# A planner that gives out all eight PSUM banks piece by piece, in a kernel of an FFT convolution and a gated MLP

## The chip, the cores and the metric

The kernel runs on one core of one Trainium2 chip. The core has five engines: TensorE (PE, with its weight loads shown apart as PEld), VectorE (DVE), ScalarE (ACT), GpSimd (POOL) and SyncE (SP, which here only issues DMAs). The metric is the device time of one execution in microseconds (us).

## The reference

Two blocks follow one another on an input u of 2048 positions and 512 channels. All is float32.

```
x   = layernorm(u)
dt  = exp(log_dt);  A = -exp(log_A_real) + 1j*A_imag
K   = 2 * real(sum_n  C[d,n]*dt[d] * exp(A[d,n]*dt[d] * l))     # a filter of 2048 taps for each of 512 channels, 128 modes n
y   = irfft(rfft(x, 4096) * rfft(K, 4096))[:2048]
h   = u + y + x * D_skip
z   = gelu(layernorm(h) @ w_in);  z1, z2 = halves of z
out = h + (z1 * (w_sp @ layernorm(z2) + b_sp)) @ w_out
```

## The kernel before, in words

The first block is `phase_a`, the second the phases `b1`, `b2` and `b3`. The change lies in `phase_a` alone.

**The work of phase a.** The 512 channels are handled in four chunks of 128. For each chunk, eight *units* (`unit`, line 619) make the filter: two matmuls give phases in PSUM (`ph`), ScalarE and VectorE reduce them to a fraction of a turn, ScalarE takes sines and cosines, GpSimd makes three products of amplitudes (`m`, in the tile `wa`), VectorE multiplies amplitudes with sines and cosines, TensorE sums over the modes, and ScalarE copies the result into `ks`. A unit's tiles appear in the profile as `f`, `ph`, `ce`, `wb` (the buffers `cs`) and `wa` (the buffers `m`).

The convolution is cut in *pieces*, eight of each kind for a chunk: `piece_a` (line 707) is the first step of the transform of the input and `piece_b` the second, whose result is `ka`; `kb` is a copy of `ka` with its halves exchanged, made by DMA. `piece_c` (line 719) is the first step of the transform of the filter, into a quarter of `big` called `x1k`. `piece_d` is the second step and multiplies it into `ka` and `kb`. It goes by groups of frequencies, so it needs all eight pieces c of its chunk. `piece_e` (line 727) is the inverse, by groups of four channels. Each piece is some matmuls into one PSUM bank and an evacuation by ScalarE (a, b, c, e) or two multiplications by VectorE (d).

Before this come `norm_x` (the layer norm: 64 normalizing operations, given out to ScalarE, VectorE and GpSimd by the string `NORM`, lines 503 to 522) and `params` (line 539: some 40 small operations on 128 x 128 elements, for chunks 0 and 1 alone and for 2 and 3 together). `table` and `stack` load what the units of the next chunk need.

**The order of the work.** `phase_a` does not issue instructions; it hands them to `Plan` (line 178) with a due time for each (`nc.at`). `Plan` has a cost for every operation, builds a list schedule, improves it by going forwards and backwards, shakes the due times at random 60 times (`TRIES`), keeps the best, and issues the instructions in that fixed order, engine by engine. A cost model of the engines stands in `_add`; it knows that VectorE and GpSimd exclude each other in some operations (`port`). All these instructions bear line 424 in the profile.

**PSUM.** It has eight banks of 512 float32 per partition. `phase_a` fixes four for `ph` (two units of two banks), one for the second cosine `ce`, and leaves three (`FFT_BUFS`) for the planner to give to pieces. The filter sums of a unit go into the first half of its `ph`.

**The hand-over.** What stands after the last use of the units' tiles is not issued in `phase_a` but by `rest`, from `phase_b1` (line 818), behind the loads of that phase. After the first inverse piece of the last chunk the weights of the next phase are split (lines 808 and 809, tiles `w1h` and `w1l`).

Of the kernel before, what the change touches and what calls it, by code (L numbers as in the profile page):

```python
# [26 lines left out]
NORM = "aavaapav"  # L27
# [4 lines left out]
TRIES = 60  # L32
# [145 lines left out]
class Plan:  # L178
# [4 lines left out]
    HOP = 0.2  # L183

    def __init__(self, nc, banks):
        self.nc, self.banks, self.ops, self.live, self.t, self.step = nc, banks, [], {}, 0.0, 0.0
        self.nbank, self.open = 0, None
        for e in self.ENGINES:
            setattr(self, e, _Engine(self, e))
# [4 lines left out]
    def bank(self, shape):  # L194

        self.nbank += 1
        n = math.prod(shape[1:])
        names = "abc"[:len(shape) - 1]
# [5 lines left out]
    def group(self, dur):  # L204

        self.open = dict(calls=[], aps=[], eng=None, dur=dur)
        yield
        g, self.open = self.open, None
        self._add(**g)

    def _resolve(self, x, bank=None):
        return x.view(self.banks[0] if bank is None else bank) if isinstance(x, Late) else x

    def call(self, e, method, args, kw, dur=None):
# [10 lines left out]
        return self._add(calls, aps, e, dur)  # L225

    def _add(self, calls, aps, eng, dur):
        e, method, args, kw = calls[0]
        o = dict(id=len(self.ops), eng=self.ENGINES[eng], calls=calls, t=self.t, deps={}, banks=set(), func=None, lat=0.0)
        self.t += self.step  # L230
        o["port"] = False
        views = [(self._resolve(x), w) for x, w in aps]
        spaces = [str(v.space) for v, _ in views]
        out, ins = views[0][0], [v for v, w in views[1:] if math.prod(v.shape[1:]) > 1]
        n = math.prod(out.shape[1:])
        isps = ["PSUM" in str(v.space) for v in ins]
        if o["eng"] == "DVE":
            ins = ins or [out]
            two = method not in ("tensor_scalar", "tensor_scalar_add", "tensor_scalar_mul", "tensor_copy", "memset", "bn_stats",
                                 "reciprocal")  # L240
            c = math.prod(ins[0].shape[1:]) if method == "bn_stats" else n
            ps = any(isps) or "PSUM" in str(out.space)
            if two or ps or method == "bn_stats":
                d = 0.15 + c / 960
            elif method == "reciprocal":
                d = 0.15 + c / 160
            else:
                d = 0.15 + c / 1920
            o["port"] = not ps and method not in ("bn_stats", "reciprocal", "memset")
        elif o["eng"] == "ACT":  # L250
            d = 0.18 + n * 0.00083
            f = str(args[2]).split(".")[-1] if method == "activation" else "Copy"
            o["func"] = {"Exp": "exp", "Sin": "sin", "Arctan": "sin"}.get(f)
        elif o["eng"] == "POOL":
            d, o["port"] = 0.3 + n * 0.0022, True
        elif o["eng"] == "PE":
            d = 0.4
        else:
            d = 0.06
        if method == "dma_start":  # L260
            nb = 4 * out.shape[0] * n if out.shape else 0
            o["lat"] = 2.0
            o["dma"] = nb / 250e3
            o["port"] = False
            if o["eng"] == "POOL":
                d = 0.7
        o["dur"] = dur if dur is not None else d
        for (x, w), (v, _) in zip(aps, views):
            key = x.key if isinstance(x, Late) else v.tensor.name
            if isinstance(x, Late):  # L270
                o["banks"].add(x.key)
            if isinstance(key, str) and key.startswith("in_"):
                continue
            self._touch(o, key, v, w)
        o["names"] = {v.tensor.name for v, _ in views}
        self.ops.append(o)
        return o
# [27 lines left out]
    def prepare(self):  # L305
# [8 lines left out]
        for ids in holders.values():  # L314
            for i in ids[1:]:
# [9 lines left out]
    def list_schedule(self, want, back=False):  # L325
# [9 lines left out]
        ready, free = {e: [] for e in engines}, {e: 0.0 for e in engines}  # L335
        est, start, end = [0.0] * n, [0.0] * n, [0.0] * n
        banks, held, until, uses = [(0.0, i) for i in range(len(self.banks))], {}, {}, dict(self.uses)
        port = dma = last = 0.0
        table = None
        for i in range(n):  # L340
            if not left[i]:
                ready[ops[i]["eng"]].append(i)
        for _ in range(n):
            best = None
            for e in engines:
                cand = []
                for i in ready[e]:
                    t = max(est[i], free[e])
                    if i in self.bank_of and self.bank_of[i] not in held:
                        if not banks:  # L350
                            continue
                        t = max(t, min(banks)[0])
                    if ops[i]["port"]:
                        t = max(t, port)
                    cand.append((t, i))
                if cand:
                    soon = min(cand)[0] + 0.25
                    w, i, t = min((want[i], i, t) for t, i in cand if t <= soon)
                    if best is None or (t, w, i) < best:
                        best = (t, w, i)  # L360
            t, _, i = best
            o = ops[i]
            e = o["eng"]
            ready[e].remove(i)
            b = self.bank_of.get(i)
            if b is not None and b not in held:
                x = min(banks)
                banks.remove(x)
                held[b] = x[1]
            d = o["dur"]  # L370
            if o["func"] and o["func"] != table:
                d, table = d + 1.28, o["func"]
            start[i], end[i] = t, t + d
            free[e] = end[i]
            if o["port"]:
                port = end[i]
            done = end[i]
            if "dma" in o:
                dma = max(dma, end[i]) + o["dma"]
                done = dma + o["lat"]  # L380
            last = max(last, done)
            if b is not None:
                uses[b] -= 1
                until[b] = max(until.get(b, 0.0), end[i])
                if not uses[b]:
                    banks.append((until[b] + self.HOP, held[b]))
            for x in after[i]:
                left[x] -= 1
                est[x] = max(est[x], done + (0.0 if ops[x]["eng"] == e and "dma" not in o else self.HOP))
                if not left[x]:  # L390
                    ready[ops[x]["eng"]].append(x)
        return last, start, end, held

    def improve(self, want, rounds):

        best = None
        for _ in range(rounds):
            last, start, end, held = self.list_schedule(want)
            if best is None or last < best[0]:
                best = (last, want, start, held)  # L400
            _, _, back, _ = self.list_schedule([-x for x in end], True)
# [3 lines left out]
    def schedule(self, tries):  # L405
        self.prepare()
        rnd = random.Random(1)
        best = self.improve([o["t"] for o in self.ops], 8)
        for _ in range(tries):
            s = rnd.choice([0.5, 1.0, 2.0])  # L410
            new = self.improve([x + rnd.gauss(0.0, s) for x in best[1]], 4)
            best = min(best, new, key=lambda b: b[0])
        last, _, start, held = best
        for o in self.ops:
            o["bank"] = held.get(self.bank_of.get(o["id"]))
        return sorted(self.ops, key=lambda o: (start[o["id"]], o["id"])), last, start

    def issue(self, o):
        def real(x):
            return x.view(self.banks[o["bank"]]) if isinstance(x, Late) else x  # L420
# [17 lines left out]
def phase_a(ctx, gen, tc, ins, cst, ident, c_mean, c_inv, Q, wp, scr):  # L438
# [12 lines left out]
    x1, kab = one(w1, "x1", [SLOT]), [one(w1, t, [SLOT]) for t in ("ka", "kb")]  # L451
# [41 lines left out]
    pm1 = Carve(kab[1])  # L493
# [8 lines left out]

    def norm_x(half, al, t0, t1):
# [5 lines left out]
        mean, rstd, nmr = group_norm(nc, al, bank, st, 32, c_mean, f"lnx{half}")  # L509
        nc.at(t1, 0.3)  # L510
        xo = big[:, 0::3, :].rearrange("p h (x l) -> p h x l", x=64)
        for j in range(32):
# [3 lines left out]
            e = NORM[j % len(NORM)]  # L516
            if e == "a":
                nc.scalar.activation(o, i, AF.Identity, bias=nmr[:, j:j + 1], scale=rstd[:, j:j + 1], dur=0.58)
            else:
                eng = nc.gpsimd if e == "p" else nc.vector  # L520
                eng.tensor_scalar(o, i, mean[:, j:j + 1], rstd[:, j:j + 1], op0=ALU.subtract, op1=ALU.mult,
                                  dur=1.05 if e == "p" else 0.47)
# [16 lines left out]
    def params(al, c0, n, rt):  # L539

        N = n * NS
# [5 lines left out]
        ai, cr, ci = (rt[:, i].rearrange("p c s -> p (c s)") for i in range(3))  # L547
        a, b, mx, mn, ph, c_, t, th = (al(N) for _ in range(8))
# [3 lines left out]
        for c in range(n):  # L552
            s_ = slice(NS * c, NS * c + NS)
            nc.scalar.activation(th[:, s_], ai[:, s_], AF.Identity, scale=ndt[:, c0 + c:c0 + c + 1])
# [7 lines left out]
        nc.scalar.activation(dummy, half_pi, AF.Sin)  # L562
# [16 lines left out]
        nc.vector.scalar_tensor_tensor(ph, pr[:, 2], -31.5, ph, op0=ALU.mult, op1=ALU.add)  # L579
        rounded(ph)  # L580
        nc.vector.scalar_tensor_tensor(pr[:, 0], t, MAGIC, ph, op0=ALU.subtract, op1=ALU.subtract)
# [587 lines left out]
```

## Time and profile before

| | us |
|---|---|
| three executions, median | 989.69 |
| lowest and highest | 985.25, 992.40 |
| the profiled execution, its own time | 990.94 |
| its span, first to last instruction | 989.2 |
| TensorE busy, of the span | 866.9 |
| VectorE | 546.4 |
| ScalarE | 397.2 |
| GpSimd | 230.1 |
| granted TensorE clock, mean | 0.974 |

Busy time is the time in which an engine has an instruction in it, and an instruction that waits for a port counts as busy. Matmuls are pipelined and their ends are modelled. In rows of groups the columns are: line, engine, operation, output<-inputs by tile, shapes, count | busy us, mean ns of one | idle time before them and what ended it. In rows of a timeline they are: start, length, engine, line, operation, shapes, count, and in brackets the idle time before.

### The profile page before, as it was taken

The page shows a single profiled execution, that of the slowest core. Times are in us where ns is not written, and L with a number is a line of the kernel's source. Part 1 is how long each engine was busy: PE and PEld are TensorE (multiplying, and loading weights), DVE is VectorE, ACT ScalarE, POOL GpSimd, SP SyncE. Part 2 cuts the span into 40 slices and gives each one's busy share as a digit, 9 for nine tenths or more (in the row PEclk, how much of TensorE's full clock was granted, in tenths as well). Part 3 has the DMA queues.
Part 4 walks back from the last instruction along what each step waited for, and adds up shares of the span by engine and source line. Part 5 has one row for each costly group of instructions (what it writes and reads, how often), then busy time and mean ns, then how long its engine had stood idle before and what let it go on. Part 6 is the DMA issues. An engine that isn't in the chain of part 4 may idle for free.

```text
span 989.2 us, 16700 instructions
## 1 busy us (share of the span) xinstructions
PE 866.9 (88%) x6936; PEld 735.0 (74%) x6936; DVE 546.4 (55%) x994; ACT 397.2 (40%) x657; POOL 230.1 (23%) x185
## 2 busy tenths in 40 slices
PE   0245798988989978889999999999999999999994
PEld 0134687867978868878889998888888888888883
DVE  6989979998669743955427783135113311431142
ACT  4287868758766723153434442122012201211110
POOL 3656575668764600000001110000000000000010
PEclk9999999989999978989999999999999999999997
DMA  9102220061040194645341113124223422332221
GB/s 343 32 17 99 63 55 2 12 143 34 10 108 12 34 338 174 181 129 138 119 159 43 32 32 107 54 66 126 65 63 96 129 59 80 88 105 64 64 64 53
DMA packets 45386, 88.84 MB, mean 90 GB/s; under 512 B 4480, under 2 KB 19712, under 8 KB 42880
## 3 DMA queue, kind: packets, MB, share of 16 engines
q1 hardware_dynamic: 43872, 85.17, 28.7%
q0 software_dynamic: 1440, 2.62, 1.0%
q8 instruction: 54, 0.88, 0.4%
q14 instruction: 20, 0.16, 0.1%
HBM read 59.99 MB, written 19.40 MB: 80 GB/s over the span
## 4 chain that ended last, share of the span: by engine, by line
PE 77%; DVE 15%; ACT 3%; issue 3%; DMA 1%; SPq 0%; DVEq 0%; ACTq 0%
PE g L1051 31%; PE fft L424 14%; PE pz L916 8%; PE pz L965 8%; PE po L1034 6%; PE ph L424 5%; DVE f L424 3%; DVE ka L424 3%; PE y L882 3%; DVE wb L424 2%; DVE big L424 2%; PE pl L1034 2%; DVE kb L424 1%; DVE wa L424 1%; DVE x L424 1%
## 5 line engine op out<-in xcount | busy, mean ns | idle before, releaser
L1051 PE MATMUL g<-wts,z 128*128 128x512 f32 x1008 | 233.0, 391 | 0.0
L1051 PEld LDWEIGHTS g<-wts,z 128*128 128x128 f32 x1008 | 189.3, 188 | 41.5
L424 POOL TENSOR_TENSOR wa<-mt 128x512 f32<-128x512 f32 x96 | 153.2, 1620 | 90.8 <-DVE wb L424 49.9
L809 DVE TENSOR_TENSOR wts<-raws,wts 128x512 fp32r<-128x512 f32 x64 | 44.1, 690 | 187.9 <-ACT wts L808 187.9
L808 ACT CAST wts<-raws 128x512 fp32r<-128x512 f32 x64 | 39.7, 621 | 255.9 <-PE g L1051 251.9
L1086 POOL TENSOR_TENSOR sums<-sums,zo 128x512 f32<-128x512 f32 x3 | 4.3, 1417 | 365.2 <-DVE sums L1081 359.2
L965 PE MATMUL pz<-w,ht 128*128 128x448 f32 x384 | 77.4, 363 | 0.0
L965 PEld LDWEIGHTS pz<-w,ht 128*128 128x128 f32 x384 | 72.0, 187 | 5.3
L916 PE MATMUL pz<-ht,w1h 128*128 128x512 f32 x224 | 71.5, 398 | 0.0
L971 POOL TENSOR_SCALAR sm<-sm 128x1 f32<-128x1 f32 x16 | 3.8, 240 | 235.2 <-DVE sm L970 235.2
L424 DVE SCALAR_TENSOR_TENSOR f<-wb,ph 128x1024 f32<-128x1024 f32 x32 | 38.7, 1217 | 31.0 <-ACT wb L424 30.8
L424 ACT COPY big<-fft 128x512 f32<-128x512 f32 x64 | 36.4, 585 | 41.2 <-PE fft L424 41.2
L424 PE MATMUL fft<-c_inv,ka 128*128 128x128 f32 x256 | 52.2, 287 | 0.8 <-DVE ka L424 0.8
L1034 PE MATMUL po<-w,gz 128*128 128x512 f32 x216 | 52.2, 396 | 0.0
L424 PE MATMUL fft<-c_inv,kb 128*128 128x128 f32 x256 | 50.3, 280 | 0.0
L916 PEld LDWEIGHTS pz<-ht,w1h 128*128 128x128 f32 x224 | 42.8, 191 | 9.6
L1034 PEld LDWEIGHTS po<-w,gz 128*128 128x128 f32 x216 | 40.6, 188 | 9.5
L916 PE MATMUL pz<-ht,w1l 128*128 128x512 f32 x112 | 44.9, 401 | 0.0
L424 DVE TENSOR_TENSOR f<-ph,wa 128x512 f32<-128x512 f32 x64 | 41.9, 681 | 1.9 <-ACT ph L424 1.5
L424 PEld LDWEIGHTS fft<-c_inv,ka 128*128 128x128 f32 x256 | 39.8, 197 | 3.3 <-issue 1.6
L424 PE MATMUL ph<-f 128*32 128x64 f32 x1024 | 23.1, 236 | 20.9 <-DVE f L424 20.9
L424 PE MATMUL fft<-big,a 128*128 128x128 f32 x256 | 37.0, 301 | 5.0 <-DVE ka L424 4.2
(162 smaller groups left out, 1581.5 us busy)
## 6 DMA issues: line engine op xcount, KB each, us to landing
raws<-in_w_sp_dram SPq DMA_DIRECT2D x64, 256.0 KB, 2.7
kb<-ka SPq DMA_DIRECT2D x8, 1024.0 KB, 11.4
g<-in_c_g_dram SPq DMA_DIRECT2D x8, 1024.0 KB, 4.9
scr_z<-zo SPq DMA_DIRECT2D x28, 256.0 KB, 2.0
big<-in_u_a_dram SPq DMA_DIRECT2D x8, 512.0 KB, 9.7
xq<-in_u_b_dram SPq DMA_DIRECT2D x4, 1024.0 KB
scr_h<-xq SPq DMA_DIRECT2D x16, 256.0 KB, 3.9
sums<-scr_z SPq DMA_DIRECT2D x16, 256.0 KB
```

The source lines that it names most:

```text
L424: r = getattr(getattr(self.nc, e), method)(*[real(x) for x in args], **{k: real(x) for k, x in kw.items()})
L808: nc.scalar.copy(hi, src)
L809: nc.vector.tensor_sub(lo, src, hi.bitcast(F32))
L882: nc.tensor.matmul(py[:, i, :], gt[:, i, r, :], qv[:, r, l0 + i], start=(r == 0), stop=(r == 1))
L916: nc.tensor.matmul(pt, w[:, q, f], ht[n][k][:, q], start=(q == 0 and i == 0), stop=(q == 3 and i == 2))
L965: nc.tensor.matmul(pt[:, :FQ], a[:, q], w2[:, b, q, f], start=(q == 0 and i == 0), stop=(q == 3 and i == 2))
L971: nc.gpsimd.tensor_scalar_add(sm[:, 14:15], sm[:, 13:14], 1e-5)
L1034: nc.tensor.matmul(pt, gz[fb][:, x, P * a:P * a + P], wo[:, y, fb, :], start=(fb == 0 and i == 0), stop=(fb == FB - 1 and i == 2))
L1051: nc.tensor.matmul(gs[fb], z2[si][:, x, f], w[:, y], start=(si == 0 and i == 0), stop=(si == 15 and i == 2))
L1086: (nc.gpsimd if fb % 2 else nc.vector).tensor_mul(gl_[fb], gl_[fb], z1)
```

## The change

- *PSUM as one pool.* All eight banks belong to `Plan`, as four tiles of two banks. A piece asks for one bank (kind 1), a unit's phases for a pair (kind 2, at most three at once), its cosines for a pair (kind 3, at most two), its filter sums for one bank (kind 0). The first filter sum waits for the cosines (`after=cosines`), so that sums and cosines can't block each other.
- *Cosines.* One operation of 1024 elements into PSUM takes the place of two of 512 into `ce` and `cs`. The products with them read PSUM.
- *Parameters.* Chunks 2 and 3 are done apart. Four of the working rows lie in a PSUM bank. The operation that loaded ScalarE's table ahead of the arc tangent is gone.
- *Norm.* Its small steps go through PSUM (`norm_small`). Each of the 64 normalizing operations goes to ScalarE or GpSimd, as the planner finds (`either`); VectorE has none.
- *Evacuations* of pieces a, b, c and e go to ScalarE or VectorE, as the planner finds.
- *Piece d* multiplies `ka` and `kb`, now one tile `kab`, in a single operation. Its matmuls write PSUM by channel, with gaps between the elements.
- *The last chunk* is split in 16, 8 and 8 channels: pieces d and e of a part need only the pieces c of its channels. A group of d has then 8, 16 and 16 matmuls of 64, 32 and 32 columns.
- *The weights* of the next phase are split behind the last chunk's seventh inverse piece, not the first.
- *The planner* has other costs (`HOP` per engine, `OVER`, durations) and eight shakings with fixed seeds (`STEPS`) instead of 60.

The core of the diff:

```diff
-NORM = "aavaapav"
-TRIES = 60
+STEPS = ((5, 0.7), (18, 1.5), (19, 3), (25, 0.7), (36, 0.3), (225, 0.7), (233, 0.7), (332, 0.3))
...
-    HOP = 0.2
+    HOP = dict(PE=0.25, DVE=0.05, ACT=0.05, POOL=0.08, SP=0.1)
+    OVER = dict(PE=0.0, DVE=0.08, ACT=0.1, POOL=0.05, SP=0.0)
...
+    def either(self, *thunks):
+        self.alts = []
+        for th in thunks:
+            th()
+        alts, self.alts = self.alts, None
+        o = self._add(**alts[0])
+        o["forms"] += [self._form(**a) for a in alts[1:]]
...
-    ph_bufs = [one(ps, f"ph{i}", [2, W]) for i in range(2)]
-    ce = one(ps, "ce", [W])
-    nc = Plan(tc.nc, [one(ps, f"fft{i}", [W]) for i in range(FFT_BUFS)])
+    nc = Plan(tc.nc, [one(ps, f"ps{i}", [2, W]) for i in range(4)])
...
+        d, z = b[:, 1:3], b[:, 3]
...
+        v = b[:, 6]
+        nc.vector.tensor_scalar_add(v, b[:, 5], 1e-5)
+        nc.vector.tensor_scalar(rstd.bitcast(I32), v.bitcast(I32), -0.5, 1597463007.0, op0=ALU.mult, op1=ALU.add)
...
+            nc.either(
+                lambda: nc.scalar.activation(o, i, AF.Identity, bias=nmr[:, j:j + 1], scale=r, dur=0.58),
+                lambda: nc.gpsimd.tensor_scalar(o, i, m, r, op0=ALU.subtract, op1=ALU.mult, dur=1.08))
...
-        a, b, mx, mn, ph, c_, t, th = (al(N) for _ in range(8))
+        w = bank("par", [P, 4, N])
+        a, t, ph, c_ = (w[:, i] for i in range(4))
+        b, mx, mn, th = (al(N) for _ in range(4))
...
-        nc.scalar.activation(dummy, half_pi, AF.Sin)
...
+        ph = nc.bank([P, 2, W], 2)
...
-        nc.scalar.activation(ce, cs[:, 1, :], AF.Sin, bias=half_pi, scale=-TWO_PI)
-        nc.scalar.activation(cs[:, 0, :], cs[:, 0, :], AF.Sin, bias=half_pi, scale=-TWO_PI)
+        co = nc.bank([P, 2, W], 3)
+        cosines = nc.scalar.activation(co, cs, AF.Sin, bias=half_pi, scale=-TWO_PI)
...
-        kp = ph[:, 0, :256].rearrange("p (d h j) -> p d h j", d=4, h=2)
+        kp = nc.bank([P, 4, 2, 32], 0)
...
-        nc.vector.tensor_mul(cs[:, 0, :], cs[:, 0, :], m[:, 2, :])
-        nc.vector.tensor_mul(m[:, 0:2, :], ce.unsqueeze(1).to_broadcast([P, 2, W]), m[:, 0:2, :])
+        nc.vector.tensor_mul(m[:, 0:2, :], co[:, 1:2, :].to_broadcast([P, 2, W]), m[:, 0:2, :])
+        nc.vector.tensor_mul(cs[:, 0, :], co[:, 0, :], m[:, 2, :])
...
+    def evac(out, src):
+        return nc.either(lambda: nc.scalar.copy(out, src, dur=0.59), lambda: nc.vector.tensor_copy(out, src, dur=0.68))
...
-    def piece_d(c, g):
-        pt = st2(x1k, g)
-        for t in ab:
-            last[1] = nc.vector.tensor_mul(of_group(t, g), by_channel(pt), of_group(t, g))
+    def piece_d(c, g, lo, n):
+        kn = P // n
+        pt = bank("s2", [P, n, kn, 4])
+        with nc.group({4: 0.95, 8: 1.2, 16: 2.0}[kn]):
+            for j in range(kn):
+                nc.tensor.matmul(pt[:, :, j, :].rearrange("p d q -> p q d"), a2v[:, kn * g + j, :], x1k[:, kn * g + j, :, lo:lo + n],
+                                 start=True, stop=True)
+        v = kab.rearrange("p i (d k) -> p i d k", d=32)[:, :, lo:lo + n, 4 * kn * g:4 * kn * g + 4 * kn]
+        last[1] = nc.vector.tensor_mul(v, pt.rearrange("p d k q -> p d (k q)").unsqueeze(1).to_broadcast([P, 2, n, 4 * kn]), v)
...
-        if s == 0:
+        if s == 6:
             last[0] = e
...
-        pieces(piece_d, c, t + 8.5 * T, t + 10.2 * T)
-        pieces(piece_e, c, t + 10.2 * T, t + 13 * T)
+        if c + 1 < NCH:
+            split = [(0, 32, 8.5)]
+        else:
+            split = [(0, 16, 5.5), (16, 8, 7.5), (24, 8, 9.0)]
+        for lo, m, at in split:
+            for g in range(m // 4):
+                nc.at(t + at * T)
+                piece_d(c, g, lo, m)
+            for s in range(lo // 4, (lo + m) // 4):
+                nc.at(t + (at + 1.7) * T)
+                piece_e(c, s)
```

More of the change, by code (lines that the diff above doesn't have):

```diff
@@ L260, in _add @@
[L260 to L268, printed above, removed]
+        ps = any("PSUM" in str(v.space) for v in ins + [out])
+        if method == "dma_start":
+            f["dma"] = 4 * out.shape[0] * n / 250e3
+            d = 0.7 if f["eng"] == "POOL" else 0.06
+        elif f["eng"] == "DVE":
+            one = ("tensor_scalar", "tensor_scalar_add", "tensor_scalar_mul", "tensor_copy", "memset")
+            if method == "reciprocal":
+                d = 0.15 + n / 160
+            elif method == "bn_stats":
+                d = 0.28
+            else:
+                d = 0.15 + n / (1920 if method in one and not ps else 960)
+                f["port"] = not ps and method != "memset"
+        elif f["eng"] == "ACT":
+            d = 0.2 + n * 0.00082 + 0.08 * any(hasattr(kw.get(k), "offset") for k in ("bias", "scale"))
+            func = str(args[2]).split(".")[-1] if method == "activation" else "Copy"
+            f["func"] = {"Exp": "exp", "Sin": "sin", "Arctan": "atan"}.get(func)
+        elif f["eng"] == "POOL":
+            d, f["port"] = 0.25 + n * 0.0025, True
+        else:
+            d = 0.4
@@ L270, in _add @@
             if isinstance(x, Late):
                 o["banks"].add(x.key)
[L272 to L277, printed above, removed]
+            if not (isinstance(key, str) and key.startswith("in_")):
+                self._touch(o, key, v, w)
     def _touch(self, o, key, v, write):
@@ L385, in list_schedule @@
                 if not uses[b]:
-                    banks.append((until[b] + self.HOP, held[b]))
+                    banks[held[b]] = until[b] + 0.05
+                    if self.wide(b):
+                        banks[held[b] + 1] = until[b] + 0.05
+                        limits[self.kinds[b]] += 1
             for x in after[i]:
                 left[x] -= 1
-                est[x] = max(est[x], done + (0.0 if ops[x]["eng"] == e and "dma" not in o else self.HOP))
+                same = len(ops[x]["forms"]) == 1 and ops[x]["forms"][0]["eng"] == e and "dma" not in f
+                est[x] = max(est[x], free[e] if same else done + self.HOP[e])
                 if not left[x]:
-                    ready[ops[x]["eng"]].append(x)
-        return last, start, end, held
+                    offer(x)
+        return last, start, end, held, took
     def improve(self, want, rounds):
@@ L713, in piece_b @@
     def piece_b(c, g):
-        nc.scalar.copy(of_group(ab[0], g), by_channel(st2(x1u, g)), dur=0.59)
+        pt = bank("s2", [P, 4, P])
+        with nc.group(0.95):
+            for j in range(4):
+                nc.tensor.matmul(pt[:, j, :], a2v[:, 4 * g + j, :], x1u[:, 4 * g + j, :, :], start=True, stop=True)
+        evac(ab[0][:, :, 4 * g:4 * g + 4, :], pt.rearrange("p k (d q) -> p d k q", q=4))
         if g == 7:
@@ L800, in rest @@
             done[o["id"]] = nc.issue(o)
-            if o is last[0]:
+            if o in last and all(x["id"] in done for x in last):
                 yield [done[x["id"]] for x in last]
```

317 lines of the change are left out of this document (174 added, 143 removed).

## The prediction

> **What bounds the kernel now.** I read the page first, for the span and for the chain that ended last.
>
> ```profile
> span 989.2 us, 16700 instructions
> ...
> PE 77%; DVE 15%; ACT 3%; issue 3%; DMA 1%; SPq 0%; DVEq 0%; ACTq 0%
> ```
>
> TensorE carries 77% of that chain, but VectorE's 15% all lies in one part of the kernel. To see it I took ScalarE's timeline and looked for the copy that ends each filter unit (`ks<-ph`). There are 32 of them, eight for each chunk of channels; these are the 8th, 16th, 24th and 32nd:
>
> ```profile
> 149.07 0.37 ACT L424 COPY ks<-ph 128x256 f32<-128x256 f32 x1 [2.08 <-PE ph L424]
> ...
> 229.89 0.37 ACT L424 COPY ks<-ph 128x256 f32<-128x256 f32 x1 [2.74 <-issue]
> ...
> 294.58 0.37 ACT L424 COPY ks<-ph 128x256 f32<-128x256 f32 x1
> ...
> 358.81 0.37 ACT L424 COPY ks<-ph 128x256 f32<-128x256 f32 x1 [6.76 <-PE ph L424]
> ```
>
> So the chunks take until 149, then 81, 65 and 64 us. I cut the trace at these points and asked for each engine's busy time in each stretch (columns: stretch, its length, then busy us and count for PE, weight loads, DVE, ACT, POOL, then clock and DMA):
>
> ```profile
> 0.00:30.00 30.00, 2.02 (x5) 0.91 (x5) 21.28 (x84) 13.53 (x27) 13.03 (x15) 1.00 0.77 287
> 30.00:149.40 119.40, 73.94 (x1119) 59.77 (x1120) 108.03 (x187) 82.36 (x144) 74.34 (x54) 0.97 0.20 54
> 149.40:230.30 80.90, 70.29 (x1073) 60.35 (x1071) 75.59 (x93) 60.60 (x87) 52.09 (x35) 0.96 0.21 49
> 230.30:295.00 64.70, 58.70 (x945) 50.96 (x946) 45.65 (x60) 48.89 (x72) 44.98 (x32) 0.97 0.24 55
> 295.00:359.20 64.20, 56.76 (x904) 49.38 (x902) 47.52 (x63) 43.20 (x64) 28.52 (x18) 0.98 0.28 78
> 359.20:393.90 34.70, 30.07 (x208) 28.61 (x208) 14.04 (x20) 8.43 (x13) 0.00 (x0) 0.79 0.64 257
> 393.90:480.00 86.10, 79.88 (x483) 71.14 (x484) 52.53 (x185) 26.90 (x53) 0.00 (x0) 0.96 0.50 138
> 480.00:989.00 509.00, 495.28 (x2206) 413.88 (x2204) 181.79 (x307) 113.28 (x201) 17.13 (x35) 0.99 0.27 79
> ```
>
> The reader is to see four limits. From 30 to 149 us VectorE is the bound (108.0 of 119.4). From 149 to 230 VectorE (75.6) and TensorE (70.3) are both close to 80.9. From 230 to 359 TensorE leads, 58.7 of 64.7 and 56.8 of 64.2. From 359 to 394 only TensorE works, at a granted clock of 0.79. From 394 on the change touches nothing; I carry those 595 us over unchanged.
>
> Why VectorE is the bound is in its groups, up to 149.4 us:
>
> ```profile
> L424 DVE TENSOR_TENSOR f<-ph,wa 128x512 f32<-128x512 f32 x20 | 13.2, 679 | 0.3 <-ACT ph L424 0.3
> ...
> L424 DVE TENSOR_SCALAR wb<-f 128x1024 int32<-128x1024 int32 x10 | 12.1, 1224 | 0.0
> ...
> L424 DVE TENSOR_TENSOR wb<-wb,wa 128x512 f32<-128x512 f32 x10 | 8.2, 833 | 0.0
> L424 DVE TENSOR_SCALAR big<-big,ka 128x128 f32<-128x128 f32 x16 | 7.4, 562 | 0.1
> ...
> L424 DVE TENSOR_SCALAR ka<-ka 128x32 int32<-128x32 int32 x2 | 6.2, 3108 | 0.0
> L424 DVE TENSOR_TENSOR x<-x 128x128 f32<-128x128 f32 x10 | 6.0, 598 | 0.1
> L424 DVE TENSOR_TENSOR big<-big 128x256 f32<-128x256 f32 x3 | 5.1, 1692 | 0.0
> L424 DVE SCALAR_TENSOR_TENSOR kb<-kb 128x128 f32<-128x128 f32 x7 | 4.6, 656 | 0.0
> ```
>
> An operation with an input in PSUM (`ph`) takes 679 ns for 512 elements. The same size with both inputs in SBUF (`wb`, `wa`) takes 833. A 128x32 operation takes 3108 ns on average. The timeline of VectorE and GpSimd shows what it waits for:
>
> ```profile
> 34.24 0.29 DVE L424 TENSOR_TENSOR kb<-kb 128x128 f32<-128x128 f32 x1
> ...
> 35.81 2.95 POOL L424 TENSOR_TENSOR wa<-mt 128x512 f32<-128x512 f32 x2
> ...
> 36.77 4.71 DVE L424 TENSOR_SCALAR ka<-ka 128x32 int32<-128x32 int32 x1
> 38.74 1.27 POOL L424 TENSOR_TENSOR mt<-mt,rcs 128x512 f32<-128x512 f32 x1
> 39.97 1.46 POOL L424 TENSOR_TENSOR wa<-mt 128x512 f32<-128x512 f32 x1
> ...
> 109.81 0.41 DVE L424 SCALAR_TENSOR_TENSOR big<-big 128x256 f32<-128x256 f32 x1
> ```
>
> The 32-element operation starts at 36.77 and ends at 41.48, just when GpSimd's row of operations ends (39.97 + 1.46 = 41.43). Undisturbed, 128 elements take 0.29 us and 256 take 0.41. So an SBUF-only operation on VectorE sits out whatever GpSimd is doing, and the busy time in the table is largely waiting.
>
> **The change, part by part.**
>
> *First stage (to 149 us), VectorE.* The 16 normalizing operations leave VectorE: 7.4 us. The norm's steps go through PSUM, so the 3108 ns operation should fall to about 0.2: 2 x 2.9 = 5.8. Parameter steps in PSUM: `x` 10 x (0.598 - 0.29) = 3.1, `kb` 7 x (0.656 - 0.29) = 2.6, `big` 3 x (1.692 - 0.41) = 3.8. The cosine product now reads PSUM: 10 x (0.833 - 0.68) = 1.5. Sum 24.2 us. The absolute value (`wb<-f`, 1224 ns) stays in SBUF and keeps its wait. Who is next? ScalarE, by these rows over the whole of the planned phase (to 395 us; the first is its share of the norm):
>
> ```profile
> L424 ACT ACTIVATE ph<-f 128x1024 f32<-128x1024 f32 x32 | 32.7, 1027 | 3.1 <-DVE f L424 2.9
> L424 ACT ACTIVATE wb<-wb 128x512 f32<-128x512 f32 x32 | 22.9, 717 | 1.5 <-DVE wb L424 1.5
> L424 ACT ACTIVATE ce<-wb 128x512 f32<-128x512 f32 x32 | 22.0, 689 | 4.3 <-DVE wa L424 2.4 <-DVE wb L424 1.6
> ...
> L424 ACT ACTIVATE big<-big,ka 128x128 f32<-128x128 f32 x40 | 18.8, 589 | 14.6 <-DVE ka L424 14.5
> ```
>
> If ScalarE takes all 16 norm operations it gains 16 x 0.589 = 9.4 us. Two cosines of 0.717 + 0.689 become one of 1024 elements into PSUM, for which the sine's 1.027 is the price: 0.38 less per unit, 3.8 over the ten here. ScalarE then has 82.4 + 5.6 = 88 us to do in 119.4 - 24 = 95. That is 92%, as full as VectorE was (90%), unless the planner gives the norm to GpSimd, which would lengthen waits again. So I take 20 of the 24. Bounds: -12, if half of the removed waiting turns up in the operations that stay in SBUF (GpSimd is busy 74.3 of 119.4), and -30, if smaller groups gain too.
>
> *Second stage (149 to 230).* Here the SBUF product is worst:
>
> ```profile
> L424 DVE TENSOR_TENSOR wb<-wb,wa 128x512 f32<-128x512 f32 x8 | 11.7, 1460 | 0.0
> ```
>
> 8 x (1.46 - 0.68) = 6.2 us off VectorE, the parameters a little more. TensorE idles only 80.9 - 70.3 = 10.6, which is the ceiling. I take -6; bounds 0 and -10.
>
> *Third stage.* TensorE is idle 6 of 64.7. I take -1; bounds 0 and -5. The 128 evacuations that may now go to either engine, and the joined multiplication (one of 1024 instead of two of 512), relieve ScalarE and VectorE, which here lie beside TensorE: nothing.
>
> *Last chunk (295 to 394).* The rows are of TensorE's timeline and of the chain of waits:
>
> ```profile
> 329.72 4.63 PE L424 MATMUL fft<-x,a 128*128 128x128 f32 x40
> ...
> 341.63 2.84 PE L424 MATMUL fft<-wb,ks 128*64 128x128 f32 x48
> ...
> 373.96 2.04 PE L424 MATMUL fft<-big,a 128*128 128x128 f32 x8 [2.43 <-DVE ka L424]
> ```
> ```profile
> 352.78 5.32 issue
> ...
> 376.79 16.50 PE fft L424 x128
> ```
> ```profile
> 381.56 3.46 ACT L808 CAST w1h<-w1r 128x896 fp32r<-128x896 f32 x4
> ```
>
> Each matmul of the code stands as two instructions. Back to back with 128 weight columns and 128 moving ones, one takes 4.63/40 = 0.116 us; with half the weights 2.84/48 = 0.059. The last chunk's spectra product had 64 of them, 7.4 us. Split in three it has 192, with 64, 32 and 32 moving columns. No row shows so short a matmul in a run; I bound one by 0.059 and 0.116 and take 0.075, half for the weights and a little for the columns, nearer the row in which half the work is gone: 14.4 us, so +7 (bounds +3.9 and +14.9).
>
> The tail, from the last unit's copy to the last evacuation, was 393.9 - 358.8 = 35 us. Now it is one forward piece (16 x 0.059 = 0.9), its copy 0.6, the product of 8 channels (64 x 0.075 = 4.8), a multiplication 1.2, two inverse pieces of 16.50/8 = 2.06, a copy 0.6 and some 0.3 of handing over: 12.5 us. At the slow pace of the row at 373.96 (2.04/8 = 0.255 per instruction, against 0.116) TensorE's part doubles and it is 22.
>
> But this isn't a gain of 12 to 22 us: what leaves the tail must be done among the units, where TensorE is full. Its work in the two last stretches is 56.8 + 30.1 = 86.8 us. About 6 of that is the slow clock (the inverse 16.5 against 128 x 0.116 = 14.8, the product some 32 instructions at 0.255 instead of 0.116), so 81, plus 7 for the split, plus some 3 in the tail in which it must wait: 91. The stall of 5.3 us in which TensorE's instructions come late ("issue") may or may not fall there again, half is 2.7. That makes 94 against 98.9 before: I take -6 with the shorter gaps between units, bounds +8 (every short matmul at 0.116, tail slow) and -12.
>
> *Weights of the next phase.* The casts of 3.46 us, which stood behind the first of eight inverse pieces and were hidden by the other seven, now stand behind the last but one, so the last copy may queue behind them: +2, bounds 0 and +3.5. One more parameter load on SP's queue is beside everything.
>
> Sum: -20 - 6 - 1 - 6 + 2 = -31. The profiled execution took 990.94 us (span 989.2); the median of three is 989.69, so the two agree within 1.3. 990.9 - 31 = 960.
>
> **The rivals.** *TensorE holds* (0.17): the first stage gives its lower bound, -12, the later ones nothing, since TensorE was their bound; with -2 for the tail the time is 977. For it: the busy shares from 230 us on. Against it: 45 us of idle TensorE in the first stage.
>
> *The new product writes PSUM with gaps, and so slowly* (0.07): each matmul of the spectra product now writes its 128 (64, 32) columns in an order that jumps over 16 or more elements. Over four chunks that is 256 x 128 = 32,768 columns, and a column now takes about (0.116 - 0.059)/128, some 0.45 ns. If a jump costs three times that on top, 1.35 ns, it is 44 us on a TensorE that is nearly full from 149 us on: 960 + 44 = 1004, slower than before. It decides from 31 us, 0.95 ns a column; a mere doubling gives 975. The only matmul of this trace that writes with gaps writes four columns, too few to price one:
>
> ```profile
> L424 PE MATMUL ph<-wb,ident 128*128 128x4 f32 x64 | 13.6, 282 | 0.0
> ```
>
> The Trainium skill, in "PSUM — Partial Sum Buffer", section "Specifications (TRN2)", states that any non-contiguous access pattern slows matmuls significantly, which is this rival and gives no figure; no run shown so far can test it. By that rule the time would lie on the slow side of the forecast; by the pace of the writes without gaps it is 960. I go by the latter, since no row speaks for a slower one, and leave the rule its chance.
>
> *Banks run short* (0.06): the units' phases, cosines and products and five kinds of pieces now share eight banks that the old kernel kept apart. If each of the 160 pieces (five kinds, four chunks, eight each) waits 0.2 us, it is 32 us and nothing is gained: 991. Against it: two units held four banks throughout, now only while they need them.
>
> *More* (0.12): with ScalarE and VectorE balanced the first two stages reach their lower bounds: -30 - 10 - 6, 945.
>
> **How the numbers follow.** The forecast has 0.58 and by itself runs from 948 to 972. About 1% is what a measurement of this kernel can tell from no change. Faster: 0.58 + 0.12 and three quarters of 0.17, 0.83. Same: the rest of that and the banks, 0.10. Slower: 0.07. The range from 938 to 983 leaves out the slow product, most of the banks and the far end of the gain.
>
> **What would show it.** Right: the 8th unit's copy near 129 us and the 32nd near 345 to 350; no VectorE operation of 32 or 128 elements over 0.5 us on average; the product of cosines at 0.68; a tail of 13 to 22 us; the product's matmuls in the first three chunks at 0.116. Wrong: the same matmuls at 0.2 or more (the gaps cost); the 8th copy still after 140 us (ScalarE took over); TensorE waiting on ScalarE's or VectorE's copies for more than before (banks).

## The result, and the profile after

The changed kernel takes 1071.88 us (median of 4 runs, 1059.7 to 1074.24) against 989.67 for the kernel before: a ratio of 1.0811 [1.072, 1.0901]. It is slower by 8%, where 960 us was forecast. The profiled execution took 1072.08 us, span 1070.3.

First a correction. ScalarE's copies that the prediction called the 8th, 16th and 24th unit's were the 10th, 18th and 25th. The 1st, 8th, 16th and 24th of the kernel before are these; the 32nd (358.81) was right:

```profile
58.80 0.37 ACT L424 COPY ks<-ph 128x256 f32<-128x256 f32 x1 [0.79 <-ACT big L424]
...
132.66 0.37 ACT L424 COPY ks<-ph 128x256 f32<-128x256 f32 x1
...
209.62 0.37 ACT L424 COPY ks<-ph 128x256 f32<-128x256 f32 x1 [3.69 <-PE ph L424]
...
287.25 0.37 ACT L424 COPY ks<-ph 128x256 f32<-128x256 f32 x1 [4.00 <-PE ph L424]
```

The same five of the changed kernel:

```profile
90.66 0.37 ACT L485 COPY ks<-ps 128x256 f32<-128x256 f32 x1 [3.42 <-issue]
...
145.53 0.38 ACT L485 COPY ks<-ps 128x256 f32<-128x256 f32 x1
...
229.52 0.37 ACT L485 COPY ks<-ps 128x256 f32<-128x256 f32 x1 [3.70 <-PE ps L485]
...
322.48 0.37 ACT L485 COPY ks<-ps 128x256 f32<-128x256 f32 x1 [0.80 <-PE ps L485]
...
406.50 0.37 ACT L485 COPY ks<-ps 128x256 f32<-128x256 f32 x1 [6.79 <-PE ps L485]
```

Cut at these points, the changed kernel's busy times are (columns as in the prediction's table):

```profile
0.00:90.70 90.70, 18.07 (x114) 11.19 (x114) 61.97 (x219) 51.56 (x114) 49.92 (x56) 1.00 0.40 139
90.70:145.50 54.80, 42.15 (x840) 34.67 (x840) 42.97 (x51) 37.60 (x51) 39.44 (x28) 1.00 0.24 54
145.50:229.50 84.00, 67.23 (x1026) 56.97 (x1026) 59.99 (x73) 51.42 (x64) 52.67 (x38) 0.97 0.18 42
229.50:322.50 93.00, 72.35 (x1072) 60.20 (x1072) 66.80 (x75) 50.42 (x62) 48.19 (x34) 0.96 0.17 40
322.50:406.50 84.00, 65.44 (x1013) 55.95 (x1013) 55.48 (x64) 40.37 (x54) 34.44 (x23) 0.99 0.25 77
406.50:474.50 68.00, 56.23 (x312) 53.83 (x312) 13.70 (x12) 9.29 (x15) 0.00 (x0) 0.66 0.27 106
474.50:1070.00 595.50, 575.80 (x2688) 485.48 (x2688) 234.17 (x492) 140.50 (x253) 17.07 (x35) 0.98 0.30 88
```

Two things are to be seen. From 145 to 406 us no engine is full any more: in the fourth row TensorE has 72 of 93 us and VectorE 67. So the time goes into waits between engines. And the tail, 35 us before, is 68 at a granted clock of 0.66. The last row is the part that the change doesn't touch: 595.5 us, as before.

VectorE's operations themselves became what was forecast:

```profile
L485 DVE TENSOR_SCALAR wb<-f 128x1024 int32<-128x1024 int32 x32 | 39.2, 1229 | 0.2
...
L485 DVE TENSOR_TENSOR kab<-ps,kab 128x1024 f32<-128x1024 f32 x32 | 37.4, 1218 | 70.3 <-PE ps L485 60.2 <-ACT wb L485 5.0 <-ACT x L485 2.6
L485 DVE TENSOR_TENSOR wb<-ps,wa 128x512 f32<-128x512 f32 x32 | 21.8, 683 | 4.1 <-ACT ps L485 4.1
...
L485 DVE TENSOR_SCALAR kab<-ps 128x32 int32<-128x32 int32 x2 | 0.4, 191 | 0.1
```

The cosine product takes 683 ns, the norm's integer step 191 instead of 3108. But the row of `kab<-ps,kab` (piece d) has 70.3 us of idle time ahead of it, 60 of them for TensorE. The list of waits up to 480 us (us in total, times, longest) says the same from both sides. First three rows of the kernel before, then the changed kernel's:

```profile
ACT big L424 <- PE fft L424: 41.2, 29, 19.2
...
DVE ka L424 <- PE fft L424: 15.4, 4, 12.1
...
PE fft L424 <- ACT big L424: 2.2, 3, 1.0
```

```profile
ACT big L485 <- PE ps L485: 94.5, 36, 24.5
DVE kab L485 <- PE ps L485: 80.3, 20, 19.9
...
PEld ps L485 <- ACT big L485: 29.1, 31, 2.7
...
PE ps L485 <- ACT big L485: 23.2, 30, 2.4
...
PE ps L485 <- ACT x L485: 17.0, 13, 7.4
PE ps L485 <- DVE kab L485: 16.4, 18, 1.4
```

TensorE waits for copies (`big`) for 23.2 us instead of 2.2, and the copies wait for TensorE for 94.5 instead of 41.2. How, the tail's timeline shows (start, length; in brackets the idle time before and what ended it):

```profile
432.15 3.65 PE L485 MATMUL ps<-c_inv,kab 128*128 128x128 f32 x16 [1.32 <-DVE kab L485]
435.83 1.22 DVE L485 TENSOR_TENSOR kab<-ps,kab 128x1024 f32<-128x1024 f32 x1 [3.74 <-PE ps L485]
437.11 2.05 PE L485 MATMUL ps<-c_inv,kab 128*128 128x128 f32 x16 [1.32 <-DVE kab L485]
439.24 0.59 ACT L485 COPY big<-ps 128x512 f32<-128x512 f32 x1 [24.50 <-PE ps L485]
439.88 2.05 PE L485 MATMUL ps<-c_inv,kab 128*128 128x128 f32 x16 [0.72 <-ACT big L485]
441.97 0.59 ACT L485 COPY big<-ps 128x512 f32<-128x512 f32 x1 [2.14 <-PE ps L485]
...
449.82 7.04 PE L485 MATMUL ps<-big,a 128*128 128x32 f32 x32 [0.68 <-ACT big L485]
```

The first inverse piece ends at 435.80. Its copy could start then, but starts at 439.24, just after the next inverse piece has ended (437.11 + 2.05 = 439.16). These two pieces lie in the two halves of one tile `ps`: the plan names the banks, and all pieces of this stretch take turns in one tile while the other three stand empty. The planner chooses so: of the free banks it prefers the one whose neighbour is in use. Pair the TensorE groups of the planned phase, by the plan's banks, with the earlier ScalarE or VectorE work on the other half of their tile: of some 240 such groups none began before that work had ended, and over 40 began within 0.25 us after, nearly all of them with their own half free for longer. So the two halves seem to exclude each other in the built program, while the plan reckons them as two; the first experiment tests it.

### The profile page after: what moved, and what is told of

Same layout as the page of the kernel before. It is cut to its first block, busy times and chain, and to the rows that moved or that the text cites. A ratio compares the mean times of both kernels' runs of the same rounds, so it can differ in the third digit from the quotient of the medians.

```text
span 1070.3 us, 16959 instructions
## 1 busy us (share of the span) xinstructions
PE 897.3 (84%) x7064; PEld 758.3 (71%) x7064; DVE 535.1 (50%) x985; ACT 381.2 (36%) x609; POOL 241.7 (23%) x210
## 4 chain that ended last, share of the span: by engine, by line
PE 53%; DVE 1%; issue 0%
PE g L1140 29%; PE pz L1005 7%; PE pz L1054 7%; PE po L1123 5%; PE y L971 3%; PE pl L1123 2%; DVE w1r L994 0%; DVE w1r L992 0%; PE lnh_pm L128 0%; DVE stats L976 0%; DVE raws L1126 0%; DVE xq L974 0%; DVE ht L898 0%; PE lnh_pv L137 0%; DVE small L132 0%
## 5 line engine op out<-in xcount | busy, mean ns | idle before, releaser
L485 POOL TENSOR_TENSOR wa<-mt 128x512 f32<-128x512 f32 x96 | 149.2, 1579 | 121.1 <-PE ps L485 60.0
L485 PE MATMUL ps<-c_inv,kab 128*128 128x128 f32 x512 | 69.5, 293 | 17.2 <-ACT big L485 7.9
L485 PEld LDWEIGHTS ps<-c_inv,kab 128*128 128x128 f32 x512 | 63.9, 204 | 22.3 <-ACT big L485 10.1
L485 DVE TENSOR_TENSOR kab<-ps,kab 128x1024 f32<-128x1024 f32 (+1 forms) x34 | 38.0, 1164 | 71.0 <-PE ps L485 60.9
L485 PE MATMUL ps<-big,a 128*128 128x128 f32 (+2 forms) x384 | 60.3, 325 | 7.2 <-ACT big L485 3.1
L485 ACT COPY big<-ps 128x512 f32<-128x512 f32 x54 | 30.7, 588 | 97.1 <-PE ps L485 94.5
L485 PEld LDWEIGHTS ps<-big,a 128*128 128x128 f32 x384 | 57.8, 241 | 10.4 <-ACT big L485 4.1
L485 PE MATMUL ps<-wb,ks 128*64 128x128 f32 x512 | 37.2, 295 | 14.2 <-ACT big L485 4.4
L485 DVE TENSOR_TENSOR f<-ps,wa 128x512 f32<-128x512 f32 x64 | 42.3, 681 | 7.8 <-ACT ps L485 7.0
```

Source lines behind the costliest of these rows:

```text
L485: r = getattr(getattr(self.nc, e), method)(*[real(x) for x in args], **{k: real(x) for k, x in kw.items()})
```

## The experiments

**Theory one:** the halves of a two-bank tile exclude each other, which costs most of the loss. **Theory two:** splitting the last chunk costs the rest, since a short matmul costs as much as a long one. **Rivals:** gapped writes; the luck of the order that the planner's search finds; the cosine in one operation. The order is searched anew in every kernel below but the first. Times are medians; ratios are to the kernel before on the same chip, with 95% intervals.

*The old kernel with four of its banks paired in tiles.*

```
-ce = one(ps, "ce", [W])
-nc = Plan(tc.nc, [one(ps, f"fft{i}", [W]) for i in range(FFT_BUFS)])
+fp = [one(ps, f"fft{i}", [2, W]) for i in range(2)]
+ce = fp[1][:, 1]
+nc = Plan(tc.nc, [fp[0][:, 0], fp[0][:, 1], fp[1][:, 0]])
```

> The kernel before, with one thing changed: the planner's three banks and the second cosine's bank are no longer four tiles of one bank but the halves of two tiles of two banks. Its plan and its instructions are the same. Theory 1 (the two halves of a two-bank tile exclude each other in the built program: an instruction on one half waits for what stands before it on the other): pieces can overlap with each other's copies only across the tiles, so the time rises by 30 to 80 us over 990, to 1020 to 1070. Theory 2 (the writes with gaps and the short matmuls of the new product cost the time) and theory 3 (the new plan's order costs it): nothing of theirs is in this kernel, 985 to 995.

1023.08 us, 1.0316 [1.0242, 1.0390]. The plan doesn't see this edit: only which banks form a tile differs, and it costs 32 us. Apart from semaphores the two built programs have the same instructions in the same order on every engine; only `ce` has the last of the eight banks instead of the fifth, and the planner's three move down by one. So theory one holds in the old kernel too, and the cause is the program's waits, not a lack of banks.

*The changed kernel, single banks spread over the tiles first.*

```
-key=lambda p: (p[1], p[0])
+key=lambda p: (not p[1], p[0])
```

> The changed kernel, with one thing changed: where the planner has a choice, a piece gets a bank of a tile whose other bank is free, instead of one whose other bank is in use. Theory 1: fewer pieces share a tile, so part of the loss comes back, 1010 to 1055 from 1072; not all, since units hold pairs and pieces must still share. Theories 2 and 3: the same product and nearly the same order, 1060 to 1080.

1045.47 us, 1.0542 [1.0491, 1.0592]: 26 less than the changed kernel, by the choice of neighbours and the order that follows from it.

*One-bank tiles for the pieces, two-bank tiles only for what needs two banks* (three of these and two single; then two and four, with the order kept at the best of 80 shakings):

```
-nc = Plan(tc.nc, [one(ps, f"ps{i}", [2, W]) for i in range(4)])
+nc = Plan(tc.nc, [one(ps, f"pp{i}", [2, W]) for i in range(3)] + [one(ps, f"ps{i}", [W]) for i in range(2)])
```

> The changed kernel with its eight banks laid out as three tiles of two banks (phases and cosines of the units only) and two tiles of one bank (pieces, sums, parameters, norm), at most two units' phases and one unit's cosines at once, and the planner told so; the list of shakings is the same, so the plan is another one. No tile is shared by two users. Theory 1: the planner's independence then holds on the chip, and the time is below 1000, some 960 to 995 (two banks for all pieces are fewer than three before). Theories 2 and 3: above 1030.

> As the run with three pairs, but two tiles of two banks (one for phases, one for cosines at a time) and four tiles of one bank, and the planner keeps the best of 80 shakings. Theory 1: 955 to 985, since pieces have four banks of their own, one more than before the change. Theories 2 and 3: above 1030.

1014.84 us, 1.0233 [1.0181, 1.0284], and 1005.83, 1.0142 [1.0088, 1.0196]. That is 57 and 66 us back, but both lie above theory one's ranges, and neither is below 1000: something else costs as well.

*The split undone:* in the changed kernel with its four tiles (e6), with two (e7) and with three two-bank tiles (e8), the latter two with the best of 80 shakings.

```
-split = [(0, 16, 5.5), (16, 8, 7.5), (24, 8, 9.0)]
+split = [(0, 32, 8.5)]
```

> The changed kernel with its four two-bank tiles, but with the last chunk's spectra and inverse in one piece of 32 channels as in the kernel before. Theory (the split costs some 15 to 25 us beside the two-bank tiles): 1047 to 1060, with the clock at 0.95 or more through the last chunk's product. Rival (the whole loss is the tiles): 1065 to 1080.

> The changed kernel with two two-bank tiles and four one-bank tiles, the order kept at the best of 80 shakings, and the last chunk in one piece of 32 channels. Theory (tiles and split together are the whole loss): 975 to 988, which is faster than before, since the DVE's longer waits of before are gone. Rival (something else of the change costs as well: the cosine in one operation that the first product now waits for, or the parameters' order): 995 or more.

> The same with three two-bank tiles and two one-bank tiles. Theory: 980 to 992, since e3_three_pairs stood at 283.6 after 24 units, as e4_two_pairs did at 282.3, and only the halves that pieces no longer use are lost. Rival (something else of the change costs as well): 998 or more.

e6: 1047.94 us, 1.0562 [1.0514, 1.0610]. e7: 989.86, 0.9989 [0.9957, 1.0020]. e8: 981.24, 0.9880 [0.9847, 0.9913]. The split is worth 24 us in the changed kernel (1071.88 - 1047.94); without it the tail is 38 us instead of 68. The tiles are worth another 67 (1047.94 - 981.24), though e8 differs from e6 also in how many pairs the units may hold at once and in how the order is chosen. e7 came 2 us above its range. e8's gain leaves little room for a large cost of the cosine in one operation, which was not tested by itself. In e8's tail the inverse no longer takes turns with its copies:

```profile
360.39 14.56 PE L483 MATMUL ps<-c_inv,kab 128*128 128x128 f32 x128 [1.32 <-DVE kab L483]
362.52 0.58 ACT L483 COPY big<-ps 128x512 f32<-128x512 f32 x1 [13.28 <-PE ps L483]
364.31 0.58 ACT L483 COPY big<-ps 128x512 f32<-128x512 f32 x1 [1.20 <-PE ps L483]
```

*The luck of the order:* the changed kernel with the best of 80 shakings (e10), and e8 with 80 others (e12).

> The changed kernel, four two-bank tiles and split as they are, with another order: the best of 80 shakings instead of eight named ones. Theory (tiles and split cost, whatever the order): 1045 to 1085. Rival (the loss is bad luck of one order): below 1035.

> The same as e8_three_pairs_one_piece, one piece of 32 channels, with 80 other shakings to choose the order from: it shows how much of a difference between two kernels is the luck of the order. Theory (the cause lies in tiles and split): 973 to 993. Rival (luck of the order is as large as what was put down to tiles and split): outside 965 to 1005.

e10: 1078.00 us, 1.0865 [1.0810, 1.0920]. e12: 976.81, 0.9842 [0.9810, 0.9874]. Another order moves the time by 6 and 4 us here, not by 82. e12 is the fastest version tried, and beats both kernels.

*The split alone, in the old kernel.* e9 splits the last chunk and keeps the layout. There the later groups' product reads values that the earlier groups' inverse has overwritten, so that e9 doesn't compute the convolution, and it has to wait for that inverse, which the split itself doesn't ask. e13 has the new layout of the spectra alone (with gapped writes), e14 the layout and the split. e9 and e14 also split the next phase's weights behind the seventh inverse piece, as the changed kernel does.

```
-x1k = big[:, 3, :].rearrange("p (k d q) -> p k d q", k=NK1, q=4)
+x1k = big[:, 3, :].rearrange("p (k q d) -> p k q d", k=NK1, q=4)
...
+            nc.tensor.matmul(pt[:, :, j, :].rearrange("p d q -> p q d"), a2v[:, kn * g + j, :], x1k[:, kn * g + j, :, lo:lo + n],
```

> The kernel before with one thing of the change: the last chunk's spectra and inverse in groups of 16, 8 and 8 channels, written to PSUM without gaps, the banks and all else as before; the work of the next phase is released by the last inverse piece but one, as in the changed kernel (the order is searched anew). Theory (the split is the second cost): it adds 128 pairs of weight load and short matmul; at two instructions of 0.112 us each pair-half, 192 instead of 64 instructions cost 14.3 us more, less some 4 us of work that now overlaps, and more where the granted clock falls to half: 1000 to 1015. Rival (the split itself is a gain, and only the two-bank tiles spoil it): 978 to 988.

> The kernel before with the changed kernel's layout of the spectra alone: each matmul of the spectra product writes its 128 columns to PSUM in an order that jumps, the multiplications read and write whole runs; no split, banks as before. Theory (gaps cost nothing, a matmul's price is its weight load): product at 0.112 us per instruction, time 984 to 998. Rival (gaps slow the writes): product at 0.15 or more, time 1005 or more.

> The same with the last chunk in groups of 16, 8 and 8 channels, so that the split stands alone in the old kernel and every group reads its own data. Theory (the split costs 128 instructions of 0.112 us, 14.3 us, less some 4 of overlap, more where short matmuls meet a halved clock): 998 to 1012. Rival (the split is a gain that only two-bank tiles spoil): 975 to 988.

e9: 999.71 us, 1.0123 [1.0082, 1.0164], just below its range, with ten times between 997.57 and 1011.37. e13: 992.30, 1.0014 [0.9995, 1.0034]: gapped writes cost nothing that shows. e14: 1006.76, 1.0163 [1.0125, 1.0202]: the split, with the weights' later place, costs 14.5 us beside e13. Its 32nd unit's copy starts 11.6 us earlier than e13's (351.93 against 363.51), but its tail is 21.2 us longer (56.3 against 35.1). The expected size is right, but not for the expected reason alone. The product's groups in the changed kernel, then in e14 (count, busy us, mean ns of one with its overlap):

```profile
L485 PE MATMUL ps<-big,a 128*128 128x32 f32 x128 | 25.0, 370 | 1.4 <-ACT big L485 1.4
L485 PE MATMUL ps<-big,a 128*128 128x128 f32 x192 | 23.8, 280 | 3.4 <-ACT big L485 1.7 <-DVE kab L485 0.8 <-ACT x L485 0.7
L485 PE MATMUL ps<-big,a 128*128 128x64 f32 x64 | 12.1, 369 | 2.4 <-issue 2.4
```
```profile
L424 PE MATMUL fft<-big,a 128*128 128x128 f32 x192 | 24.9, 282 | 0.0
L424 PE MATMUL fft<-big,a 128*128 128x32 f32 x128 | 24.4, 369 | 0.0
L424 PE MATMUL fft<-big,a 128*128 128x64 f32 x64 | 13.3, 399 | 0.0
```

Going by these means, a matmul of 32 columns takes longer than one of 128, but the means mix two clocks. From start to start, one takes 0.112 us with 128, 64 and 32 columns alike where the clock is full (e9 has all three), and 0.213 to 0.215 in these runs of short ones. e14's stretches, with the granted clock as third number from the end, and TensorE's timeline in the second:

```profile
300.00:351.90 51.90, 46.95 (x786) 40.66 (x786) 39.95 (x48) 33.92 (x54) 24.50 (x15) 1.00 0.31 85
351.90:408.20 56.30, 54.87 (x336) 54.23 (x336) 13.76 (x20) 8.79 (x14) 0.00 (x0) 0.67 0.35 142
```
```profile
359.59 27.52 PE L424 MATMUL fft<-big,a 128*128 128x64 f32 x128
```

TensorE is busy for 54.87 of 56.30 us, yet the clock is 0.67: 128 matmuls, of 64 and of 32 columns in turns, run back to back for 27.5 us at 0.215 apiece (27.52/128).

*Two halves of 16 channels, on e8.*

```
-split = [(0, 32, 8.5)]
+split = [(0, 16, 7.0), (16, 16, 9.0)]
```

> Three two-bank tiles and two one-bank tiles, as in e8_three_pairs_one_piece, with the last chunk in two halves of 16 channels: 128 instructions of 64 columns instead of 64 of 128. Theory (a matmul's price is its weight load, so each further group adds 7.2 us to TensorE, and the granted clock can fall under short matmuls): 983 to 1000, slower than e8's 981. Rival (the overlap that a split allows outweighs the 7.2 us, and only the groups of 8 channels cost): 968 to 978.

997.18 us, 1.0054 [1.0032, 1.0076]: 16 us above e8 and inside the theory's range, in part by luck. Its 128 matmuls ran at 0.112 each, which is 7.2 us more for TensorE. But of the 22.5 us between the two profiled executions 13 are there before the last chunk: the 24th unit's copy starts at 284.57 against 271.63. The edit doesn't touch that part; there the order alone differs, which was searched anew. So at a single point the order can move the time by more than the 4 to 6 us above.

*The free choice of engine for the copies undone, on e8.*

```
-return nc.either(lambda: nc.scalar.copy(...), lambda: nc.vector.tensor_copy(...))
+return nc.scalar.copy(out, src, dur=0.59)
```

> As e8_three_pairs_one_piece, but the evacuations of the pieces may go to ScalarE alone, as in the kernel before; VectorE loses its 32 of them, 22 us. Theory (VectorE's gain was spent on these evacuations, and it is VectorE that sets the first two chunks): 965 to 977. Rival (they were free where VectorE did them, and ScalarE becomes the bound): 985 or more.

998.10 us, 1.0078 [1.0055, 1.0101]: the rival's range. VectorE's 32 copies had not eaten the gain: without them the kernel is 17 us slower than e8. The 24th unit's copy starts at 301.88 instead of 271.63, so the loss comes before the last chunk. How much of it is the new order isn't shown; in e11 that was 13 us at the same place.

## Why the prediction was wrong

**Banks.** The failed step is that eight banks count as eight: outside the rivals the prediction put the wait of one piece for another's copy at nothing. In its tail the inverse pieces stand back to back at 2.06 us with only the last copy, 0.6, behind them; in the trace four of the eight wait 0.7 us or more for the copy of the piece before. The prediction's rival "Banks run short" named the right engines to look at, but priced 160 pieces at 0.2 us of scarcity and gave it 0.06. It isn't scarcity: e1 pairs banks that the old kernel kept apart and loses 32 us. In the changed kernel exclusion costs some 67 us (e6 against e8). The full diff showed where to look: the tiles of `[2, W]`, and the choice that prefers a bank with a busy neighbour.

**First and second stage, -20 and -6.** The durations held (683 and 191 ns above); the times didn't follow. With tiles repaired and no split, the 24th unit ends at 271.6 (e8) or 277.3 us (e12) instead of 287.2: 10 to 16 us for the forecast 27. So even repaired the kernel takes 977 to 981 us, not 960. The absolute value, said to keep its wait, rose from 1000 to 1229 ns in the changed kernel. The 1st unit came later, not earlier (68.8 and 80.3 us against 58.8). Why is left open.

**Third stage, copies at nothing.** Probably wrong: without the choice of engine e15 is 17 us slower once the tiles are repaired, though the order has an unknown part in it.

**Last chunk, -6.** The mis-sized term is the split's +7, from 0.075 us a matmul. The row of 0.059 from which it came has half the weight columns; the split leaves the weights whole and narrows the moving columns. Measured are 0.112, so 128 more of them are +14.3 us, close to the upper bound of +14.9. What no bound held is the slow clock over the whole product, which the prediction had allowed in the tail alone: at 0.213 the 192 take 41 us. The split, with the weights' later place, cost 14.5 us in the old kernel (e14 against e13), and the split 24 in the changed one; the tail forecast at 12.5 to 22 was 68, and 56.3 in e14.

**Gapped writes.** This rival fell: 0.112 us per matmul and e13's 1.0014. Its 0.45 ns a column was no column's price, since the two rows that it was taken from differ in weight columns; with 128, 64 and 32 moving columns alike at 0.112, a somewhat slower write could stay hidden, but not one of 0.2 us. The Trainium skill, "PSUM — Partial Sum Buffer", section "Specifications (TRN2)", states that any non-contiguous access pattern slows matmuls significantly; these runs don't show it for such writes.

**Casts, +2.** Right: in e8 the inverse ends at 374.95 and its last copy starts at 377.04, behind the casts. In the changed kernel the last inverse piece waits for a copy that stands behind them, 1.79 us where its neighbour's wait is 0.72, so that 1.1 us are theirs:

```profile
467.48 2.05 PE L485 MATMUL ps<-c_inv,kab 128*128 128x128 f32 x16 [0.72 <-ACT big L485]
...
471.32 2.05 PE L485 MATMUL ps<-c_inv,kab 128*128 128x128 f32 x16 [1.79 <-ACT big L485]
```

**The rest** (595 us) was carried over rightly.

## What to carry to other kernels

Before you count buffers, ask at what grain the program tracks them: two halves of one tile may be one buffer, and a planner that doesn't know it can make each engine wait for the other. Look in the trace for what a matmul's price follows: here it was the weight columns (0.112 us with 128, whether 32 or 128 columns moved, and 0.059 with 64). Then splitting work into narrower pieces is priced by the number of matmuls that it adds. A sum of shorter durations is a gain only while the order that fills the engines survives; look at where the first and last piece of each stage land.

## What was not expected of the hardware

Narrow matmuls lost the full clock although TensorE didn't idle. In e9 the two last parts have 64 matmuls of 32 columns each, back to back. This is the first of the two runs, and then the stretches of both:

```profile
364.54 9.45 PE L424 MATMUL fft<-big,a 128*128 128x32 f32 x64
```
```profile
364.40:372.00 7.60, 7.60 (x72) 7.51 (x60) 1.29 (x2) 0.37 (x1) 0.00 (x0) 0.83 0.96 346
382.00:390.00 8.00, 7.85 (x56) 7.85 (x56) 1.29 (x2) 0.10 (x1) 0.00 (x0) 0.78 0.00 0
```

In the first run the starts are 0.112 us apart until 369.5 and 0.213 after, with no gap: after 5 us the clock halves. In the second it halves after 4.3 us, with no DMA running, so the DMA share of 0.96 in the first isn't the cause. Those of 64 columns kept it in e11 (80 in 9.14 us), but didn't raise it once it had fallen: in e4 it stood at half through 20 us of unbroken narrow ones, 64 columns first and then 32, and came back 3.3 us after full inverse matmuls had begun (364.24):

```profile
343.70:354.10 10.40, 10.40 (x51) 10.40 (x51) 4.62 (x4) 1.66 (x2) 0.00 (x0) 0.50 0.95 384
354.10:364.60 10.50, 10.50 (x77) 10.27 (x77) 7.03 (x9) 1.34 (x2) 0.00 (x0) 0.50 0.06 23
...
367.50:373.00 5.50, 5.50 (x51) 5.50 (x51) 0.00 (x0) 1.76 (x3) 0.00 (x0) 1.00 0.00 0
```

The Trainium skill, "TensorE: Matmul & The Clock Gate", section "What's actually happening", gives full clock after one busy window of some 3.4 us. The traces come near it for full-width matmuls (3.3 us in e4, 4.0 for the inverse and 5.3 for the product in the kernel before); for narrow ones 20 us of unbroken work was not enough.
